# Head 1's last score product on the whole array, and every engine's order of instructions as a table

## The chip, the cores and the metric

The kernel runs on one core of one Trainium2 chip. The core's engines each work through their own queue of instructions in order: TensorE (PE) does matrix products into the accumulation memory PSUM, its weight loads are shown apart (PEld); VectorE (DVE), ScalarE (ACT) and GpSimd (POOL) do elementwise work and reductions; SyncE (SP) issues the DMA transfers. The metric is the device time of one execution in microseconds (us), the median of several runs; lower is better.

## The reference

Attention with queries pooled in twos, and then two projections multiplied with each other and projected back, on the attention's output as tokens:

```python
# batch, heads, sequence, head width = 4, 8, 1152, 64; tokens 2304 x 512; d_ff = 1536
q_pool = q.reshape(B, H, S // 2, 2, D).mean(axis=3)
scores = 1.0 / np.sqrt(D) * np.matmul(q_pool, k.transpose(0, 1, 3, 2))
scores = scores - np.max(scores, axis=-1, keepdims=True)
attn = np.exp(scores)
attn = attn / (np.sum(attn, axis=-1, keepdims=True) + 1e-09)
x = np.matmul(attn, v).transpose(0, 2, 1, 3).reshape(B * 576, 512)
out = ((x @ w_a) * (x @ w_b)) @ w_out
```

## The kernel before

**Tiling.** Heads are worked on in 16 pairs, four to a batch. Head 0 of a pair lies on partitions 0 to 63, head 1 on 64 to 127, so the scores of the two heads (64 deep) are products on the two row halves of PE's array. 128 queries of one head against 1152 keys are a *block*; there are 144. A *round* is the two blocks of a pair for the same 128 queries (the 64 queries that are left over in a pair make a round of their own, one block for both heads). Batch 0 goes through its pairs twice (first 256 queries of each pair, then the rest), batches 1 to 3 once: 20 passes with 80 rounds, 16 of which are such leftovers. In batches 0 and 1 scores are f32 products (line 563). In batches 2 and 3 (`ps_.split`) k and q are scaled and split into a high and a low f16 part (`k_hi`, `k_lo`, `q_hi`, `q_lo`), and each score is the sum of three f16 products (line 566).

**Scores in PSUM.** `sps` has five banks of 512 columns. Head 0's 1152 scores take the first two banks and 128 columns of the third; head 1's 1024 later keys take the last two banks and its first 128 keys another 128 columns of the third. The third bank is thus shared. `qk` does a round's five larger pieces in one task (512 and 512 for each head, 128 for head 0). Head 1's remaining 128 keys, piece (1, 3), are a task of their own, `qk_rest`, which waits (`after=(ps_.last_max,)`, line 635) until DVE has read head 0's scores (`sm_max`, line 593). A switch `whole` for doing it inside `qk` stands in `scores`, always False.

**A block after its scores.** `sm_max` (DVE, line 593, scaling and maximum), `sm_exp` (ACT, 600), `sm_sum` and `sm_rec` (DVE, 604 and 610), `sm_hi` (ACT, 613) and `sm_lo` (DVE, 617) make high and low f16 parts of the probabilities; a DMA transposes them (SP, 623); `pv` (PE, 652) multiplies them with v on column halves of the array. `x_copy`, `x_hi`, `x_lo` and `x_scale` (661, 682, 686, 692) bring the result into the form that the expert layers read.

**Expert layers.** Tokens are in nine groups t of 256: two for each batch, and group 8 from the leftovers of all batches. For each of 12 slices f of d_ff, `moe_mm` (730) makes two sums of 12 f16 products on the whole array, `moe_a` and `moe_g` (737, 742) scale and multiply them, `moe_gh` and `moe_gl` (747, 750) split the result into two f32r parts, and `moe_o` (756) does the output products on the whole array. Weights are loaded and split during the first four passes, staged in the tiles `z_t`, of which the third is `z2`.

**The order.** Nothing is issued where it stands. `add` records each piece as a task with its engine, a modelled duration, a key, what it reads and writes, and for PE a `mode` (0 whole array, 1 row halves, 2 column halves, 3 output products). `Plan.order` then runs a model of the five engines, picks the ready task with the lowest key, and repeats this after random shifts of the keys (`STEPS`, 63 settings); the tasks are emitted in the order of their modelled starts. On the chip every engine keeps that order, and semaphores do the waiting.

Of the kernel before, what the change touches and what calls it, by code (L numbers as in the profile page):

```python
# [56 lines left out]
STEPS = (  # L57
# [19 lines left out]
class Plan:  # L77
# [9 lines left out]
    def add(self, eng, dur, key, fn, args=(), r=(), w=(), gen=0.45, block=0.0, port=None, lag=0.0, after=(), mode=0):  # L87
# [14 lines left out]
        self.tasks.append((ENGINES.index(eng), dur, key, fn, args, sorted(deps), gen, block, eng == "POOL" if port is None else port, lag, mode))  # L102
        return n

    def run(self, key, back):

        eng, dur, lat, out, left, gen, block, port, lag, mode = self.back if back else self.forth
        n = len(eng)
        left = list(left)
        ready_at = [0.0] * n  # L110
        start = [0.0] * n
        free = [0.0] * len(ENGINES)
        dma_free = port_free = 0.0
        last = 0
        busy = {}
        waiting = [[] for _ in ENGINES]
        ready = [([], [], [], []) for _ in ENGINES]
        push, pop = heapq.heappush, heapq.heappop
        for i in range(n):
            if not left[i]:  # L120
                push(waiting[eng[i]], (0.0, i))
        for _ in range(n):
            best = None
            for e in range(len(ENGINES)):
                rd, q = ready[e], waiting[e]
                t = free[e]
                if q:
                    if not any(rd) and q[0][0] > t:
                        t = q[0][0]
                    while q and q[0][0] <= t:  # L130
                        i = pop(q)[1]
                        push(rd[port[i] if e != PE else mode[i]], (key[i], i))
                if e == PE:
                    from_ = min((x for x in rd if x), key=lambda x: x[0][0] - PE_STAY * (x is rd[last]), default=None)
                elif rd[1] and (not rd[0] or port_free <= t and rd[1][0] < rd[0][0]):
                    t, from_ = max(t, port_free), rd[1]
                else:
                    from_ = rd[0]
                if from_ and (best is None or t < best[0]):
                    best = (t, e, from_)  # L140
            t, e, from_ = best
            i = pop(from_)[1]
            t = max(t, ready_at[i])
            d = dur[i]
# [7 lines left out]
            else:  # L152
                end = t + d
                if e == PE:
                    if mode[i] != last:
                        d += PE_TURN
                        last = mode[i]
                    end = t + d
                    tick, at = int(t / PE_TICK), t
                    while True:  # L160
# [9 lines left out]
                        at = tick * PE_TICK  # L170
                free[e] = end
            start[i] = t
            le = lat[e]
            for j in out[i]:
                x = end + le[eng[j]]
                if x > ready_at[j]:
                    ready_at[j] = x
                left[j] -= 1
                if not left[j]:
                    push(waiting[eng[j]], (ready_at[j], j))  # L180
# [793 lines left out]
```

## Time and profile before

| | |
|---|---|
| median of 3 runs | 871.57 us (870.22 to 873.34) |
| profiled execution | 872.21 us, span from first to last instruction 870.4 us |
| mean granted PE clock | 0.947 of full speed |
| busy: PE, DVE, ACT, POOL | 782.0, 648.1, 577.3, 257.0 us |
| chain that ended last | PE 17% of the span, everything else 0% |

A profile is one execution. Busy time of an engine is the time in which one of its instructions ran; matrix products are pipelined, so those of PE overlap a little, and the time that a piece of work takes from PE is better read from its start to the start of what comes next. A timeline merges neighbouring instructions of one kind into one row with their count (x24). An f32 product shows as two instructions.

### The profile page before, as it was taken

How to read it: one execution, taken by the hardware profiler on the slowest of the kernel's cores; microseconds unless marked ns; L12 is line 12 of the kernel's file. 1: busy time of each engine (PE TensorE's matmuls, PEld its weight loads, DVE VectorE, ACT ScalarE, POOL GpSimd, SP SyncE). 2: the span in 40 equal slices, each digit the busy share in tenths (PEclk: the TensorE clock that was granted, in tenths of full speed). 3: DMA queues.
4: the chain of work that ended last, by engine and by line, in shares of the span. 5: the costliest groups of instructions: out<-in, count | busy, mean ns of one | idle time of the engine just before them, and what ended most of it. 6: DMA issues, size and time to landing. Idle time of an engine off the chain costs nothing. (4 is left out here: it accounts for less than half of the span.)

```text
span 870.4 us, 21299 instructions
## 1 busy us (share of the span) xinstructions
PE 782.0 (90%) x8832; PEld 588.2 (68%) x8832; DVE 648.1 (74%) x1240; ACT 577.3 (66%) x917; POOL 257.0 (30%) x228
## 2 busy tenths in 40 slices
PE   4665538999999999999999999999999999999997
PEld 2443315777667676678777777787778768888886
DVE  5999999989778889899888999898885763122010
ACT  5789787878767677777677787776774653233212
POOL 4459876520311102221031205210520221210303
PEclk9765757999999999999999999999999999999999
DMA  7999999899999999997989999988694564000100
GB/s 275 236 237 262 239 256 232 209 188 216 218 207 205 205 168 186 196 216 146 183 165 210 174 172 208 174 180 165 137 195 77 85 130 84 2 26 1 25 1 25
DMA packets 353665, 141.76 MB, mean 163 GB/s; under 512 B 338208, under 2 KB 340256, under 8 KB 353568
## 3 DMA queue, kind: packets, MB, share of 16 engines
q1 hardware_dynamic: 353568, 140.40, 80.2%
q8 instruction: 69, 1.13, 0.6%
q14 instruction: 28, 0.23, 0.1%
HBM read 50.72 MB, written 4.72 MB: 64 GB/s over the span
## 5 line engine op out<-in xcount | busy, mean ns | idle before, releaser
L730 PEld LDWEIGHTS <-wab 128*128 128x128 f16 x2592 | 249.2, 98 | 38.1 <-issue 1.8
L730 PE MATMUL ab<-xt,wab 128*128 128x256 f16 x2304 | 266.6, 274 | 1.7 <-DVE g L742 1.0
L617 DVE SCALAR_TENSOR_TENSOR p<-s,st,p 128x1152 f16<-128x1152 f32 x144 | 209.6, 1464 | 24.3 <-ACT p L613 23.9
L600 ACT ACTIVATE s<-s,st 128x1152 f32<-128x1152 f32 x144 | 180.0, 1250 | 66.9 <-DVE s L593 66.3
L613 ACT ACTIVATE p<-s,st 128x1152 f16<-128x1152 f32 x144 | 177.7, 1246 | 30.1 <-DMA pt<-p 17.4
L750 POOL TENSOR_TENSOR gl<-g,gh 128x256 fp32r<-128x256 f32 x108 | 90.2, 838 | 334.9 <-ACT gh L747 313.6
L563 PE MATMUL sps<-k,q 64*128 64x512 f32 (+3 forms) x480 | 124.6, 596 | 41.5 <-DVE s L593 31.6
L756 PE MATMUL ab<-wo,gh 128*128 128x512 f32 x432 | 141.6, 409 | 4.5 <-DVE g L742 2.4
L652 PE MATMUL xps<-pt,vs 128*64 128x128 f16 (+1 forms) x4320 | 126.4, 217 | 8.7 <-DMA pt<-p 5.6
L563 PEld LDWEIGHTS sps<-k,q 64*128 64x128 f32 (+1 forms) x480 | 58.7, 206 | 105.6 <-issue 57.9
L652 PEld LDWEIGHTS <-vs 128*64 128x64 f16 x4320 | 115.2, 112 | 21.9 <-issue 17.1
L737 ACT ACTIVATE g<-ab,cc 128x256 f32<-128x256 f32 (+1 forms) x144 | 55.6, 415 | 87.5 <-PE ab L730 87.2
L742 DVE SCALAR_TENSOR_TENSOR g<-ab,cc,g 128x256 f32<-128x256 f32 (+1 forms) x144 | 55.9, 411 | 77.5 <-ACT g L737 77.4
L593 DVE TENSOR_SCALAR_CACHE_REDUCE s<-sps,ksc 128x1152 f32<-128x1152 f32 x72 | 101.6, 1411 | 10.8 <-PE sps L566 10.7
L593 DVE TENSOR_SCALAR_CACHE_REDUCE s<-sps 128x1152 f32<-128x1152 f32 x72 | 97.0, 1348 | 13.3 <-PE sps L563 12.9
L756 PEld LDWEIGHTS ab<-wo,gh 128*128 128x128 f32 x432 | 77.5, 189 | 24.4 <-ACT gh L747 2.2
L756 PE MATMUL ab<-wo,gl 128*128 128x512 f32 x216 | 86.2, 399 | 0.1
L747 ACT ACTIVATE gh<-g 128x256 fp32r<-128x256 f32 x108 | 43.8, 411 | 53.1 <-PE ab L756 47.8
L566 PE MATMUL sps<-k,q 64*128 64x512 f16 (+3 forms) x720 | 76.4, 325 | 2.0 <-DVE s L593 1.9
L566 PEld LDWEIGHTS <-q 64*128 64x128 f16 (+1 forms) x720 | 36.5, 97 | 45.9 <-issue 16.4
L313 POOL TENSOR_TENSOR q<-qraw 128x576 f32<-128x576 f32 (+2 forms) x20 | 31.8, 1592 | 93.6 <-DVE q L350 30.3
L467 POOL TENSOR_SCALAR xt<-xt 128x512 f16<-128x512 f32 x22 | 53.1, 2413 | 20.4 <-ACT xt L463 19.2
(93 smaller groups left out, 613.7 us busy)
## 6 DMA issues: line engine op xcount, KB each, us to landing
vraw<-in_v_dram SPq DMA_DIRECT2D x19, 576.0 KB, 4.7
k<-in_k_dram SPq DMA_DIRECT2D x19, 576.0 KB, 4.8
xt<-in_w_ab_dram SPq DMA_DIRECT2D x15, 512.0 KB, 5.0
qraw<-in_q_dram SPq DMA_DIRECT2D x12, 576.0 KB, 4.9
out_dram<-o SPq DMA_DIRECT2D x16, 256.0 KB, 2.5
xt<-in_w_out_dram SPq DMA_DIRECT2D x7, 512.0 KB, 5.2
g<-in_w_ab_dram SPq DMA_DIRECT2D x5, 512.0 KB, 5.2
pt<-p SPq DMA_TRANSPOSE x144, 5.4
```

Of the source, the lines that this page charges most:

```text
L563: nc.tensor.matmul(out, qs[jq][rows, queries], kn[jk][rows, keys], start=True, stop=True)
L566: nc.tensor.matmul(out, qf[rows, hq - 1, queries], kf[rows, hk - 1, keys], start=(hq, hk) == (1, 1), stop=(hq, hk) == (2, 1),)
L593: nc.vector.tensor_scalar(out=s_t[sbuf(i)], in0=sps[:, at:at + S], scalar1=-1.0 / 16.0 if u is None else ksc[:, u, 4:5], scalar2=None, op0 ...
L600: nc.scalar.activation(out=s, in_=s, func=AF.Exp, scale=-1.0, bias=t[:, 0:1], accum_out=t[:, 1:2])
L613: nc.scalar.activation(out=p_t[pbuf(i)][:, 0], in_=s_t[sbuf(i)], func=AF.Copy, scale=st_t[i % NST][:, 3:4])
L617: nc.vector.scalar_tensor_tensor(out=p[:, 1], in0=s, scalar=st_t[i % NST][:, 3:4], in1=p[:, 0], op0=ALU.mult, op1=ALU.subtract)
L652: nc.tensor.matmul(xps[half(e), at:at + w], vs[:, c, e, hv], pt[:, hp, c, c0:c0 + w], start=(c == 0 and n == 0), stop=(c == NCH - 1 and n ...
L730: nc.tensor.matmul(dst if t < 8 else dst.rearrange("p (b n) -> p b n", b=B), wab[:, f, 1 - m, a, c], moe_x(t, b, c), start=(n == 0), stop= ...
L737: nc.scalar.activation(out=g_t[:, f, c], in_=ab[j][:, 1, c], func=AF.Copy, scale=cc[:, b, f, 0:1])
L742: nc.vector.scalar_tensor_tensor(out=g, in0=ab[j][:, 0, c], scalar=cc[:, b, f, 1:2], in1=g, op0=ALU.mult, op1=ALU.mult)
L750: nc.gpsimd.tensor_tensor(out=gl_t[j], in0=g_t[:, f], in1=gh_t[j].bitcast(F32), op=ALU.subtract)
L756: nc.tensor.matmul(acc[u], g[:, us], wo[:, f, a], start=(first and n == 0), stop=(last and n == 2))
```

## The change

Three things. First, in batches 1 to 3 `ps_.whole` is true, and for rounds of 128 queries head 1's first 128 keys are multiplied inside `qk`, as its last piece, on the whole array: the stationary operand is all 128 rows of q (both heads), the moving one a tile `kz` whose rows 0 to 63 are zero and whose rows 64 to 127 hold head 1's keys. The separate tasks for piece (1, 3) remain in batch 0 only. Second, what `kz` needs: two buffers within `z2`, cleared once on POOL after the weights (`kz_zero`), and one copy on ACT for each of 12 passes (`k_pad`). Third, `STEPS` and the search at build time are gone; `ORDERS` lists for each of PE, DVE, ACT, POOL and SP its tasks by number, in the order in which that engine is to do them; the numbers are those of the tasks in the order of the `add` calls. A task has a second mode, `leaves`, that is 0 for a round that ends on the whole array; the model with it now only merges the five lists.

```diff
-STEPS = (
-    (64937, 0.5, 225, 20, 2), (12302, 2.0, 678, 160, 1), (13399, 8.0, 513, 40, 2), (29057, 2.0, 604, 160, 2),
...
+ORDERS = (
+    (
+        13, 6, 21, 30, 38, 140, 148, 29, 157, 48, 165, 50, 67, 267, 94, 275, 121, 156, 284, 175, 292, 177, 394, 194,
...
+    def order(self):
+        n = len(self.tasks)
+        eng, dur, _, _, _, deps, gen, block, port, lag, mode, leaves = map(list, zip(*self.tasks))
...
+            for e, o in enumerate(ORDERS):
+                if pos[e] < len(o) and not left[o[pos[e]]]:
+                    i = o[pos[e]]
+                    t = max(free[e], ready_at[i], port_free if port[i] else 0.0)
+                    if best is None or t < best[0]:
+                        best = (t, e, i)
...
+    kz = [z_t[2][:, 128 * j:128 * j + 128] for j in range(2)]
+    kzf = [x.bitcast(F16).rearrange("p (a n) -> p a n", a=2) for x in kz]
...
+    def qk(ps_, rows, rest):
         pair = rows[0][2] == 128
...
+        whole = ps_.whole and pair
+        products = ((0, 0), (0, 1), (1, 0)) if ps_.split else (None,)
+        q, k, z = (qf, kf, kzf[ps_.z]) if ps_.split else (qs[ps_.jq], kn[ps_.jk], kz[ps_.z])
+        runs = [((0, 0), (1, 0)), ((0, 1), (1, 1)), ((0, 2),)] if pair else [[(0, m), (1, m)] for m in range(3)]
+        for run in [((1, 3),)] if rest else runs:
...
+        if whole:
+            c = rows[1][1]
+            for split in products:
+                product(sps[:, S_AT[1]:S_AT[1] + 128], split, q[:, ..., c:c + 128], z)
+
+    def kz_zero():
+        for x in kz:
+            nc.gpsimd.memset(x[half(0)], 0.0)
+
+    def k_pad(ps_):
+        if ps_.split:
+            nc.scalar.activation(out=kzf[ps_.z][half(1)], in_=kf[half(1), :, 0:128], func=AF.Copy)
+        else:
+            nc.scalar.activation(out=kz[ps_.z][half(1)], in_=kn[ps_.jk][half(1), 0:128], func=AF.Copy)
...
     def scores(ps_, i, rows, rest):
-        r, whole = kq_names(ps_), False
+        whole = ps_.whole and rows[0][2] == 128
+        r = kq_names(ps_) + [f"kz{ps_.z}"] * whole
         if not rest:
-            add("PE", (1.47 if ps_.split else 1.97) + whole * (0.16 if ps_.split else 0.3), i - 8, qk,
-                (ps_, rows, ps_.jk, ps_.jq, whole), r=r, w=["sps0", "sps1"], mode=1)
+            add("PE", (1.47, 1.73)[whole] if ps_.split else (1.97, 2.37)[whole], i - 8, qk, (ps_, rows, False), r=r,
+                w=["sps0", "sps1"], mode=1, leaves=0 if whole else 1)
         elif not whole:
-            add("PE", 0.16 if ps_.split else 0.3, i - 9, qk_rest, (ps_, rows, ps_.jk, ps_.jq), r=r, w=["sps1"],
+            add("PE", 0.16 if ps_.split else 0.3, i - 9, qk, (ps_, rows, True), r=r, w=["sps1"],
                 after=(ps_.last_max,), mode=1)
...
+            self.whole = b > 0
...
+        if ps_.whole and (ps_.split or not ps_.again):
+            add("ACT", 0.19, ps_.base - 8, k_pad, (ps_,), r=["kn1", "kn1l"] if ps_.split else [f"kn{ps_.jk}"], w=[f"kz{ps_.z}"])
...
+                if m == W_PASSES:
+                    add("POOL", 0.4, ps_.base, kz_zero, (), w=["z2", "kz0", "kz1"], port=False)
```

## Rows read from the trace of the kernel before

**Rows 1.** The page's first part: busy us (share of span) and instructions of PE.

```profile
PE 782.0 (90%) x8832; PEld 588.2 (68%) x8832; DVE 648.1 (74%) x1240; ACT 577.3 (66%) x917; POOL 257.0 (30%) x228
```

**Rows 2.** Windows: stretch; length, busy PE PEld DVE ACT POOL; PE clock, DMA, GB/s.

```profile
0.00:25.00 25.00, 9.44 (x26) 4.72 (x26) 14.33 (x28) 14.46 (x20) 12.85 (x11) 0.90 0.80 276
...
100.00:125.00 25.00, 9.46 (x92) 5.78 (x86) 24.86 (x55) 21.99 (x34) 19.65 (x10) 0.73 1.00 240
...
150.00:175.00 25.00, 23.79 (x307) 17.39 (x305) 23.51 (x53) 21.28 (x36) 12.93 (x9) 1.00 0.85 225
...
325.00:350.00 25.00, 23.39 (x298) 16.59 (x295) 23.05 (x40) 18.15 (x27) 5.69 (x6) 1.00 1.04 172
```

**Rows 3.** The chain that ended last, in order of time: start us, us, what.

```profile
816.91 31.60 PE ab L730 x288
...
849.58 17.08 PE ab L756 x72
```

**Rows 4.** Timeline of PE in batch 1: start, us, line, out<-in, shapes, count.

```profile
256.88 0.48 PE L563 MATMUL sps<-k,q 64*128 64x128 f32 x2
257.30 2.79 PE L730 MATMUL ab<-xt,wab 128*128 128x256 f16 x24
260.02 2.20 PE L563 MATMUL sps<-k,q 64*128 64x512 f32 x10
262.15 1.70 PE L652 MATMUL xps<-pt,vs 128*64 128x128 f16 x54
```

**Rows 5.** Timeline of PE in batch 2.

```profile
494.33 2.79 PE L730 MATMUL ab<-xt,wab 128*128 128x256 f16 x24
497.06 0.34 PE L566 MATMUL sps<-k,q 64*128 64x128 f16 x3
497.33 1.70 PE L652 MATMUL xps<-pt,vs 128*64 128x128 f16 x54
```

**Rows 6.** Groups by form, weight loads: shapes, count, busy us, mean ns, idle before.

```profile
L730 PEld LDWEIGHTS <-wab 128*128 128x128 f16 x2592 | 249.2, 98 | 38.1 <-issue 1.8 <-DVE g L742 1.0
...
L756 PEld LDWEIGHTS ab<-wo,gh 128*128 128x128 f32 x432 | 77.5, 189 | 24.4 <-ACT gh L747 2.2 <-issue 2.1 <-DVE g L742 1.4
...
L566 PEld LDWEIGHTS <-q 64*128 64x128 f16 x576 | 29.6, 94 | 39.3 <-issue 15.0 <-DVE st L604 0.4 <-ACT gh L747 0.2
```

**Rows 7.** Timeline of PE: separate products of head 1, with idle time and releaser.

```profile
289.26 0.49 PE L563 MATMUL sps<-k,q 64*128 64x128 f32 x2 [1.04 <-DVE s L593]
...
480.11 0.33 PE L566 MATMUL sps<-k,q 64*128 64x128 f16 x3 [0.52 <-DVE s L593]
```

**Rows 8.** Groups by form: copies of 64 columns, on ACT and on POOL.

```profile
L682 ACT ACTIVATE xr<-x 128x64 f16<-128x64 f32 x16 | 4.0, 249 | 0.2
...
L686 POOL TENSOR_TENSOR xr<-x,xr 128x64 f16<-128x64 f32 x16 | 7.1, 444 | 95.5 <-ACT xr L682 95.5
```

**Rows 9.** PE's waits from 200 us on: first, third, last of ten groups.

```profile
PE xps L323 <- ACT x L661: 3.2, 3, 1.4
...
PE ab L756 <- ACT gh L747: 2.0, 1, 2.0
...
PE ab L730 <- ACT o L764: 0.4, 1, 0.4
```

**Rows 10.** Timeline of PE and, last row, of DVE where the third group starts.

```profile
370.00 1.63 PE L566 MATMUL sps<-k,q 64*128 64x512 f16 x15
...
374.31 2.79 PE L730 MATMUL ab<-xt,wab 128*128 128x256 f16 x24
...
373.68 0.34 DVE L692 TENSOR_SCALAR xt<-xt,vsc 128x512 f16<-128x512 f16 x1
```

**Rows 11.** Timeline of PE: the first expert products and the fourteenth round.

```profile
142.55 2.72 PE L730 MATMUL ab<-xt,wab 128*128 128x256 f16 x12
...
150.21 2.20 PE L563 MATMUL sps<-k,q 64*128 64x512 f32 x10
```

**Rows 12.** The page's groups: DVE's subtraction in the softmax.

```profile
L617 DVE SCALAR_TENSOR_TENSOR p<-s,st,p 128x1152 f16<-128x1152 f32 x144 | 209.6, 1464 | 24.3 <-ACT p L613 23.9
```

More of the change, by code (lines that the diff above doesn't have):

```diff
@@ L101, in add @@
         deps.discard(n)
-        self.tasks.append((ENGINES.index(eng), dur, key, fn, args, sorted(deps), gen, block, eng == "POOL" if port is None else port, lag, mode))
+        self.tasks.append((ENGINES.index(eng), dur, key, fn, args, sorted(deps), gen, block, eng == "POOL" if port is None else port, lag, mode, mode if leaves is None else leaves))
         return n
[L105 to L112, printed above, removed]
-        dma_free = port_free = 0.0
[L114 to L122, printed above, removed]
-            best = None
[L124 to L144, printed above, removed]
@@ new lines, in order @@
+    def order(self):
+        n = len(self.tasks)
+        eng, dur, _, _, _, deps, gen, block, port, lag, mode, leaves = map(list, zip(*self.tasks))
+        assert all(eng[i] == e for e, o in enumerate(ORDERS) for i in o) and sorted(i for o in ORDERS for i in o) == list(range(n))
+        out = [[] for _ in range(n)]
+        for i in range(n):
+            for d in deps[i]:
+                out[d].append(i)
+        left = [len(x) for x in deps]
+        ready_at, start = [0.0] * n, [0.0] * n
+        free, pos = [0.0] * len(ENGINES), [0] * len(ENGINES)
+        dma_free = port_free = 0.0
+        last, busy, result = 0, {}, []
+        while len(result) < n:
+            best = None
+            for e, o in enumerate(ORDERS):
[4 more added lines that the diff above has]
+                        best = (t, e, i)
+            t, e, i = best
+            pos[e] += 1
+            result.append(i)
+            start[i], d = t, dur[i]
@@ L156, in run @@
                         d += PE_TURN
-                        last = mode[i]
+                    last = leaves[i]
                     end = t + d
@@ L558, in pbuf, with product @@
         return i % NPB
-    def product(out, split, jk, jq, rows, queries, keys):
+    def product(out, split, q, k):
         if not split:
-            nc.tensor.matmul(out, qs[jq][rows, queries], kn[jk][rows, keys], start=True, stop=True)
+            nc.tensor.matmul(out, q, k, start=True, stop=True)
         else:
             hq, hk = split
-            nc.tensor.matmul(
-                out, qf[rows, hq - 1, queries], kf[rows, hk - 1, keys],
-                start=(hq, hk) == (1, 1), stop=(hq, hk) == (2, 1),
-            )
@@ L571, in products @@
-    def products(ps_):
-        return ((1, 1), (1, 2), (2, 1)) if ps_.split else (None,)
-    def qk(ps_, rows, jk, jq, whole):
-        pair = rows[0][2] == 128
-        runs = [((0, 0), (1, 0)), ((0, 1), (1, 1)), ((0, 2),), ((1, 3),)] if pair else [[(0, m), (1, m)] for m in range(3)]
-        for run in runs if whole or not pair else runs[:3]:
-            qk_run(ps_, rows, jk, jq, pair, run)
-    def qk_rest(ps_, rows, jk, jq):
-        qk_run(ps_, rows, jk, jq, True, ((1, 3),))
-    def qk_run(ps_, rows, jk, jq, pair, run):
-        for split in products(ps_):
-            for j, m in run:
-                e, c, w = rows[j]
-                cuts, at, part = (S_CUT[e], S_AT[e], slice(0, 128)) if pair else (S_CUT[0], S_AT[0], half(e))
-                a, b = cuts[m:m + 2]
-                product(sps[part, at + a:at + b], split, jk, jq, half(e), slice(c, c + w), slice(a, b))
+            nc.tensor.matmul(out, q[:, hq], k[:, hk], start=(hq, hk) == (0, 0), stop=(hq, hk) == (1, 0))
@@ new lines, in qk @@
+    def qk(ps_, rows, rest):
+        pair = rows[0][2] == 128
+        whole = ps_.whole and pair
[4 more added lines that the diff above has]
+            for split in products:
+                for e, m in run:
+                    _, c, w = rows[e]
+                    cuts, at, part = (S_CUT[e], S_AT[e], slice(0, 128)) if pair else (S_CUT[0], S_AT[0], half(e))
+                    a, b = cuts[m:m + 2]
+                    product(sps[part, at + a:at + b], split, q[half(e), ..., c:c + w], k[half(e), ..., a:b])
+        if whole:
+            c = rows[1][1]
+            for split in products:
+                product(sps[:, S_AT[1]:S_AT[1] + 128], split, q[:, ..., c:c + 128], z)
@@ L857, in more @@
         ps_.end = len(blocks)
+        ps_.z = 0 if not passes else passes[-1].z if again and not ps_.split else 1 - passes[-1].z
         passes.append(ps_)
```

44 lines of the change are left out of this document (13 added, 31 removed), and 155 rows, old and new, of tables (ORDERS, STEPS).

## The prediction

> **What bounds the kernel now.** I read the page's header first, then busy time by stretch, then the chain of work that ended last, then TensorE's (PE's) order of work, and its waits. PE is busy for 782.0 of 870.4 us [rows 1]. The reader should see two regimes. In the first 150 us PE is half idle and VectorE (DVE) is not: from 100 to 125 us DVE is busy 24.86 of 25 us, PE 9.46 us at a mean granted clock of 0.73 [rows 2]. From 150 us on PE is nearly gapless at clock 1.00: 23.79 of the 25 us after 150, and 23.39 of those after 325, with DVE at 23.05 [rows 2]. The chain that ended last runs on PE through the last groups of the expert layers, 31.60 us of first products and then, a gap of about 1 us later, 17.08 us of output products [rows 3]. So after 150 us every microsecond of PE's own work that goes away is one of the end, as long as DVE, which has only 8% free in the middle, keeps up; before that, a shorter PE is worth nothing.
>
> **The change part by part.** Two edits go together: 48 small score products are done in another way, and every engine's order is new.
>
> *The turns of PE.* What stands in the rows is a cost of changing the form of the array. Products of the expert layers on the whole array run at 31.60 us for 288, that is 0.110 us each [rows 3]. Of these, 24 between an island of scores and a score round take from 257.30 to 260.02, 2.72 us, where 24 x 0.1097 = 2.63 were due: 0.09 us is the turn [rows 4]. In the f16 batches the same 24 take from 494.33 to 497.06, 2.73 us: 0.10 us [rows 5]. I take 0.092 for each turn. Following PE's instructions from the first product to the last and counting where the form changes (whole array; scores on row halves; values on column halves; output products, whose operands are f32r), I get 353 turns before; [rows 4, 5] show seven of them. After: the table's numbers are tasks in the order in which the add calls make them, so PE's row of the table can be read task by task. It has 220 turns between tasks and one inside each of the 48 score rounds that now end on the whole array, 268. That is 85 fewer, 85 x 0.092 = 7.8 us. The reason is plain in [rows 4, 5]: all 48 products of head 1's last 128 keys in batches 1 to 3 stand alone between work of another form (256.88, 497.06), paying a turn in and a turn out. Now they end their round: 32 of the 48 rounds are followed by whole-array work, which needs no turn out.
>
> *The products themselves.* Removed: 16 in f32, each from 256.88 to 257.30 = 0.42 less the turn out, 0.33 us [rows 4]; 32 in f16, three products each, 497.06 to 497.33 = 0.27 less the turn, 0.18 us [rows 5]. Together 16 x 0.33 + 32 x 0.18 = 11.0 us. Added are as many with 128 rows of weights instead of 64, same 128 columns. The trace has no such product, so it is bounded. Below: stream alone, half of the 0.110 us that 256 columns cost, three times, 0.16 us in f16; for f32 the round of 1152 columns takes 260.02 to 262.15 less a turn, 2.04 us, so 128 columns 0.23 us [rows 3, 4]: 8.8 us in all. Above: each weight load in series with its stream, 98 ns + 55 ns three times = 0.46 us, and two loads of 189 ns + 0.23 = 0.61 us in f32 [rows 6]: 24.5 us. The nearest row is the removed product itself: same moving columns and data types, and its loads are hidden, since three loads of 94 ns mean would alone take 0.28 us and the three products take 0.18 [rows 5, 6]. So I take 11.0 and the exchange is worth nothing by itself (-2.2 to +13.5 us).
>
> The Trainium skill, "TensorE: Matmul & The Clock Gate", Part 3 (The mechanism), speaks against the change: it has a weight load overlap products in flight only where the row groups differ, which a whole-array load never has. By that rule the sum takes the upper price, the second rival below; the trace does not bear it out where whole-array products of 256 columns follow one another, at 0.110 us with a load of 98 ns each [rows 3, 6].
>
> *Their waits.* Head 1's last product had to wait until DVE had read head 0's scores from the shared bank. After 200 us that shows twice on PE, 1.04 us at 289.26 and 0.52 us at 480.11 [rows 7]: 1.6 us that go. Nothing new is late in their place: the round already waits for both heads' reads, and the second read can follow the first at once.
>
> *Pads.* Twelve new copies on ScalarE (ACT) of 64 partitions by 128 (f32) or 256 (f16) elements; the nearest row is a copy of 64 columns, 249 ns [rows 8], so 12 x 0.25 = 3 us of an engine with 293 us free. Queued behind each are exponentials and copies of the softmax, and the first round of its pass waits for it; PE meanwhile has expert-layer products, which I let cover it. Without that cover, and with ACT waiting for DVE's split of k in eight passes, it is 3 to 5 us. GpSimd's two clears of 64 x 128 (nearest: 444 ns for 128 x 64 [rows 8]) wait for the last weight staged in z2. Behind them on POOL are a sum of q and the low halves of x for batch 0; POOL is the idlest engine. Nothing on either, 0.9 us (two clears) if the start of batch 1 waits for it. SyncE issues the same 256 transfers, and the DMA engines' work is unchanged.
>
> *The new order.* PE's row holds the same interleaving with small shifts: expert work ahead of each score round (12 first products at 0.110 us a task; 17.08 / 12 = 1.42 us an output task [rows 3]) differs by under 3 us for most of the 80 rounds, by 7 at the most. At the start it goes the other way: the table puts no expert product ahead of the fourteenth round, where the trace has them from 142.55 us and the round at 150.21 [rows 11], and two more DVE subtractions of the softmax (1.46 us each [rows 12]) and one more maximum of about that length, but one shorter weight subtraction less, ahead of the first multiplication of the expert layers (`moe_g`): some 4 us of DVE time; by the eighth of these the two orders stand within 1 us. So I count the first 150 us as even (-3 to +4). Later, PE's waits from 200 us on sum to 14.7 us in ten groups [rows 9]. Less the 1.6 counted, 13.1 are left; a new order can take all of them or add as many. I take 2.0, the longest single wait of the ten groups.
>
> *Sum.* The profiled execution took 872.2 us (span 870.4). 872.2 - 7.8 - 1.6 - 2.0 = 860.8. The median of the runs, 871.57, lies 0.6 below the profiled execution, so the forecast is 860.2 us.
>
> **The rivals.** (A) *PE waits for attention instead.* At 374.31 PE starts the third group of expert layers right after DVE's scaling of its input at 373.68 [rows 10]: the store of expert work from batch 0 has just run out, and every later batch has such a hand-over. If attention is set by DVE and its queue there, PE's saving only widens the gap, and what is left is the 1.6 us: 872.2 - 1.6 - 0.6 = 870.0. For: DVE at 92% [rows 2]. Against: it is PE that was busy up to the hand-over, and head 1's maximum no longer waits for PE.
>
> (B) *Slower: whole-array weight loads are not hidden.* Place: the end of each of the 48 rounds; price +13.5 us as above: 872.2 - 7.8 - 1.6 + 13.5 - 0.6 = 875.7. It decides from 0.20 us more per round on (9.4 / 48). Against it are the two rows named.
>
> (C) *The order itself is worth more.* If half of the other waits go (6.5 instead of 2.0) and the start gains 3 us, where in the first 25 us DVE is busy only 14.33 [rows 2], it is 860.2 - 7.5 = 852.7. Against: DVE is full by 100 us, and an order written from modelled times leaves waits where the chip differs.
>
> **How the numbers follow.** Forecast 0.68, A 0.14, B 0.08, C 0.10. The forecast's own spread is 854.5 to 866 (order -4 to +6 about it). 80% needs some of A and C: 853 to 869. Faster by over 0.3% (under 869, about what a measurement can tell): forecast, C and the part of A that loses only some of the saving, 0.81; within 0.3%: 0.11; slower: B, 0.08.
>
> **What would show it.** Right: no score product of 128 columns stands alone after batch 0; expert products before a round's end keep 0.110 us; the rounds of batches 2 and 3 grow from 1.6 [rows 10] to about 1.9 us with the inner turn and whole product, and those of batch 1 from 2.1 to about 2.5 [rows 4]; PE's busy time falls by some 8 us; the clock is 1.00 from 150 us on. Wrong: rounds over 2.0 us in f16 (B); PE gaps of several us before the third, fifth and seventh group with DVE as releaser (A); the first expert product later than 146 us (the start); waits after 200 us that sum to over 15 us (the order).

## The result and the profile after

The changed kernel takes 851.38 us, median of 4 runs (850.55 to 853.44), against 871.52 before: a ratio of 0.9771, 95% interval 0.9745 to 0.9797. That is 20.1 us less, where the prediction had 11.4 less and a range from 853 to 869; the time lies just below the range, nearest to rival C (852.7). The profiled execution took 852.03 us, its span is 849.8.

Header and windows of the changed kernel, columns as in [rows 1, 2]; the last window is longer:

```profile
PE 771.8 (91%) x8832; PEld 591.2 (70%) x8832; DVE 644.9 (76%) x1240; ACT 580.9 (68%) x929; POOL 255.1 (30%) x230
...
100.00:125.00 25.00, 10.21 (x32) 4.72 (x30) 24.30 (x56) 22.24 (x34) 19.43 (x10) 0.68 0.92 217
150.00:175.00 25.00, 23.09 (x310) 17.90 (x308) 22.03 (x45) 18.57 (x33) 17.28 (x10) 1.00 0.99 245
325.00:350.00 25.00, 25.00 (x306) 17.83 (x303) 22.42 (x44) 18.59 (x30) 8.02 (x11) 1.00 1.06 194
250.00:720.00 470.00, 468.13 (x6002) 364.38 (x6002) 400.85 (x735) 349.04 (x534) 93.85 (x107) 1.00 0.92 171
```

PE's busy time is 10.2 us lower than in [rows 1]. The first 175 us look as they did. What is new comes later: from 325 to 350 us PE has no gap at all (23.39 before), and from 250 to 720 us 1.9 us of gaps in 470. The same window of the kernel before, for comparison, left 10.5:

```profile
250.00:720.00 470.00, 459.49 (x5867) 346.30 (x5866) 401.87 (x733) 340.76 (x511) 94.10 (x104) 1.00 0.93 171
```

Note the counts: in the same 470 us PE does 135 more products (6002 against 5867).

PE's waits after the change, from 200 us to the end: engine, line, what it waited for; us in total, times, longest:

```profile
PE ab L830 <- DVE g L842: 2.1, 1, 2.1
PE ab L856 <- DVE g L842: 1.7, 2, 1.3
PE sps L657 <- issue: 1.0, 1, 1.0
PE xps L752 <- DMA pt<-p: 0.7, 1, 0.7
```

Four groups and 5.5 us stand where [rows 9] had ten groups and 14.7 us. Between 250 and 720 us only the last two are left.

The new rounds on PE, one of batch 1 (f32) and one of batch 2 (f16): start, us, line, out<-in, shapes, count:

```profile
288.05 2.17 PE L657 MATMUL sps<-k,q 64*128 64x512 f32 x10 [0.97 <-issue]
290.16 0.49 PE L657 MATMUL sps<-z,q 128*128 128x128 f32 x2
290.48 4.09 PE L830 MATMUL ab<-xt,wab 128*128 128x256 f16 x36
...
558.11 1.63 PE L660 MATMUL sps<-k,q 64*128 64x512 f16 x15
559.67 0.34 PE L660 MATMUL sps<-z,q 128*128 128x128 f16 x3
559.85 4.09 PE L830 MATMUL ab<-xt,wab 128*128 128x256 f16 x36
```

The products on the whole array (128*128) end their round, and expert products follow at once. From start to start the two f32 pieces take 0.32 us (290.16 to 290.48) and the three f16 pieces 0.18 us (559.67 to 559.85): what the separate products of [rows 4, 5] took without their turns, 0.33 and 0.18. The 36 expert products behind them start 0.112 us apart (559.85 to the next round at 563.88), turn included.

The chain that ended last, share of the span by engine, first after and then, in a fence of its own, before:

```profile
PE 53%; DVE 2%; DMA 1%; issue 1%; ACT 0%
```

```profile
PE 17%; ACT 0%; DVE 0%; issue 0%; DVEq 0%
```

Before, the chain can be followed back only to 712.63 us, the last 18% of the span. After, it goes back through more than half of it, nearly all on PE. The second line was on the page when the prediction was made.

**Where the 20 us went.** To see this I priced PE's tasks: each kind by the time from its start to the next task's start where PE is gapless, and 0.093 us for each change of array form. The rest of the span is idle time (in the first 150 us it includes the lower clock). The transfer records give the moment at which the last of the 144 transposes of probabilities has landed, which is when attention has nothing more to fetch.

| | span | PE's work | last transpose landed | PE's work left then | idle ahead of it | idle behind it |
|---|---|---|---|---|---|---|
| before | 870.4 | 739.1 | 730.4 | 133.0 | 124.3 | 7.0 |
| after | 849.8 | 731.2 | 731.9 | 111.8 | 112.5 | 6.1 |

Attention ends at nearly the same time in both. What differs is how much expert work is still to be done then: 21.2 us less, and 21.2 - 1.5 + 0.9 = 20.6, the difference of the spans. By these prices the 21.2 us come from ahead of the landing: 7.9 us were turns and are now work, 11.8 us were idle and are now work, 1.5 us are the later landing.

The table is an account, not a cause. The same sum comes out at any moment behind which PE has hardly a gap, and PE does not wait for the last landing in either kernel: it takes up the last two products with v at 746.41 and 751.03 us before, behind 288 first products without a gap, and at 726.57 and 736.79 us after. Nor does PE's row move 21 us of expert work. When the last score round starts, at 711.29 us before and 695.91 after, about 147 and 143 us of expert products are left (counted in the traces, 0.109 us for a first and 0.237 for an output product). Some 4 us are thus the row's, and 15.4 us are PE getting there sooner. What tells the kernels apart is how long attention can hold PE up. PE's last listed wait for it, before (a timeline row, then the chain):

```profile
711.29 1.62 PE L566 MATMUL sps<-k,q 64*128 64x512 f16 x15 [1.39 <-DVE s L593]
...
714.88 31.60 PE ab L730 x288
746.48 1.63 PE xps L652 x54
```

And after (the chain; the wait is the 0.7 us for a transpose in the list above):

```profile
371.85 6.33 DMA pt<-p
378.18 0.04 issue
378.22 1.67 PE xps L752 x53
```

Before, PE waits for attention here and there up to 711 us. After, it does so up to 378 us; the three waits listed from there on lie within the expert layers.

### The profile page after: what moved, and what is told of

Its sections match the earlier page's. It is cut to its first block, busy times and chain, and to the rows that moved or that the text cites. A ratio compares the mean times of both kernels' runs of the same rounds, so it can differ in the third digit from the quotient of the medians.

```text
span 849.8 us, 21268 instructions
## 1 busy us (share of the span) xinstructions
PE 771.8 (91%) x8832; PEld 591.2 (70%) x8832; DVE 644.9 (76%) x1240; ACT 580.9 (68%) x929; POOL 255.1 (30%) x230
## 4 chain that ended last, share of the span: by engine, by line
PE 53%; DVE 2%; DMA 1%; issue 1%; ACT 0%
PE ab L830 24%; PE ab L856 14%; PE sps L660 8%; PE xps L752 7%; DMA pt<-p 1%; DVE p L716 1%; DVE s L692 1%; DVE g L842 0%; ACT g L837 0%; PE xps L485 0%; DVE vs L518 0%; DVE vmx L481 0%; DVE o L862 0%; PE xps L418 0%; DVE st L709 0%
## 5 line engine op out<-in xcount | busy, mean ns | idle before, releaser
L830 PEld LDWEIGHTS <-wab 128*128 128x128 f16 x2592 | 252.4, 98 | 35.2 <-issue 2.3
L830 PE MATMUL ab<-xt,wab 128*128 128x256 f16 x2304 | 262.3, 274 | 3.2 <-DVE g L842 3.2
L716 DVE SCALAR_TENSOR_TENSOR p<-s,st,p 128x1152 f16<-128x1152 f32 x144 | 206.7, 1439 | 20.1 <-ACT p L712 19.4
L850 POOL TENSOR_TENSOR gl<-g,gh 128x256 fp32r<-128x256 f32 x108 | 94.0, 877 | 328.9 <-ACT gh L847 295.0
L657 PE MATMUL sps<-k,q 64*128 64x512 f32 (+3 forms) x448 | 117.5, 620 | 56.5 <-DVE s L692 36.6
L657 PEld LDWEIGHTS sps<-k,q 64*128 64x128 f32 (+1 forms) x448 | 54.0, 210 | 118.8 <-issue 62.9
L752 PEld LDWEIGHTS <-vs 128*64 128x64 f16 x4320 | 117.8, 113 | 19.3 <-issue 16.0
L856 PEld LDWEIGHTS ab<-wo,gh 128*128 128x128 f32 x432 | 77.8, 188 | 20.1 <-ACT g L837 1.5
L660 PE MATMUL sps<-k,q 64*128 64x512 f16 (+3 forms) x624 | 65.4, 341 | 0.0
L856 PEld LDWEIGHTS ab<-wo,gl 128*128 128x128 f32 x216 | 40.6, 188 | 10.1 <-POOL gl L850 0.4
```

The costliest lines, as they stand in the source:

```text
L657: nc.tensor.matmul(out, q, k, start=True, stop=True)
L660: nc.tensor.matmul(out, q[:, hq], k[:, hk], start=(hq, hk) == (0, 0), stop=(hq, hk) == (1, 0))
L716: nc.vector.scalar_tensor_tensor(out=p[:, 1], in0=s, scalar=st_t[i % NST][:, 3:4], in1=p[:, 0], op0=ALU.mult, op1=ALU.subtract)
L752: nc.tensor.matmul(xps[half(e), at:at + w], vs[:, c, e, hv], pt[:, hp, c, c0:c0 + w], start=(c == 0 and n == 0), stop=(c == NCH - 1 and n ...
L830: nc.tensor.matmul(dst if t < 8 else dst.rearrange("p (b n) -> p b n", b=B), wab[:, f, 1 - m, a, c], moe_x(t, b, c), start=(n == 0), stop= ...
L850: nc.gpsimd.tensor_tensor(out=gl_t[j], in0=g_t[:, f], in1=gh_t[j].bitcast(F32), op=ALU.subtract)
```

## The experiments

Ratios are against the kernel before, on the same chip and with 95% intervals; "against the change" is the difference to 0.9771, taken of 871.5 us. "Old order" is the order of the kernel before, engine by engine, written down as a table. The kernels that keep the old tasks are made from the source of the change with `whole` false and a table for these tasks. Landing, work left and span are from each kernel's own profiled execution, which can lie up to 5 us off its median.

### Each part alone

*The products alone*: the change's `qk`, pads and clears, with the old order of every engine (the 48 separate products dropped from PE's row). PE's row of the table:

```diff
-        402, 411, 419, 221, 248, 283, 619, 302, 305,
+        402, 411, 221, 419, 248, 619, 283, 302, 628,
...
```

> The old order of every engine, unchanged, with the 48 separate products of batches 1 to 3 taken out and head 1's last piece done on the whole array at the end of its round; the 12 pads stand ahead of their pass's first round. Theory 1 (the table removed PE's waits; the whole-array product only saved turns): PE's work falls by 7.9 us and the two waits of the separate products go, but the other waits after 250 us stay, so about 862 us. Theory 2 (the whole-array product removed the waits, because head 1's maximum no longer waits for PE and attention gets ahead of PE): nearly all of the change's gain, 852 to 855 us, with the table adding little. Theory 3 (the old order does not fit the new tasks): waits on the pads, no gain or a loss, 868 us or more.

Measured: 872.76 us, 1.0024 (1.0001 to 1.0048). No gain. Its waits on PE from 250 to 720 us, the four largest groups of thirteen:

```profile
PE xps L726 <- DMA pt<-p: 5.1, 5, 1.8
PE xps L392 <- ACT x L735: 2.4, 2, 1.7
PE sps L634 <- DVE s L666: 2.1, 2, 1.7
PE sps L631 <- DVE s L666: 2.0, 4, 0.6
```

PE's work did fall by 4.4 us at the prices above (739.1 to 734.7; 304 turns, since the old neighbours of a round are mostly of another form), and its idle time rose by 6.8. PE arrives earlier at the products with v and waits there for the transposes: 5.1 us, where the same wait before the change was 0.9 us. This is rival A's mechanism, and in the old order it takes everything.

*The order alone*: the table of the change with the old 48 separate products, each put into PE's row where the changed kernel's trace shows head 0's maximum to be done. Where the table takes head 1 ahead of head 0, the two products keep their old sequence.

```diff
-            self.whole = b > 0
+            self.whole = False
```

> The table's order with the old score method: the 48 products separate again, each placed in PE's row where the trace of the changed kernel shows head 0's maximum to be done; no pads; where the table reads head 1 first, head 0 first. Theory 1 (the table removed the waits): the changed kernel's time plus the 7.9 us of turns plus a few us of waits of the separate products, 859 to 864 us. Theory 2 (the whole-array product removed them): 867 us or more, with the waits after 250 us back at the old 14 us or so.

Measured: 901.01 us, 1.0331 (1.0292 to 1.037). PE's waits from 200 us on, the three largest groups:

```profile
PE sps L635 <- DVE s L667: 11.2, 12, 1.8
PE ab L805 <- DVE g L817: 8.2, 6, 2.6
PE sps L632 <- DVE s L667: 7.8, 5, 3.6
```

The order doesn't fit the old tasks. PE hardly waits at the separate products (64x128); it waits at the next rounds (64x512) until DVE has read the scores. The f16 groups by form, 200 to 900 us (busy us, mean ns; idle before):

```profile
L635 PE MATMUL sps<-k,q 64*128 64x512 f16 x384 | 47.7, 380 | 8.0 <-DVE s L667 7.9
L635 PE MATMUL sps<-k,q 64*128 64x128 f16 x192 | 21.5, 219 | 0.7 <-DVE s L667 0.7
```

That the late second product delays head 1's maximum, and this the next round, is argued from it. The places of the 48 products were chosen for this run, and others were not tried. So it doesn't price the order by itself; together with the run before it shows that in these forms neither part gains anything without the other.

### What a microsecond of PE's work is worth in either order

*The whole-array pieces done twice and left out* (in the second one head 1's first 128 keys of batches 1 to 3 get no scores), both in the change:

```diff
-        if whole:
+        for _ in range(2 * whole):
```

```diff
-        if whole:
+        for _ in range(0 * whole):
```

> The changed kernel with each of the 48 whole-array pieces done twice, the second over the first; nothing else differs. Added on PE are 32 x 0.18 + 16 x 0.32 = 10.9 us. Theory 1 (PE alone sets the time after 150 us and the order has no slack): all of it shows, about 862 us. Theory 2 (attention's chain through DVE and ACT sets parts of it): well under half shows, 851 to 856 us.

> The changed kernel without the 48 whole-array pieces: the scores of head 1's first 128 keys in batches 1 to 3 are not computed, everything else stays, in the changed order. PE loses 32 x 0.18 + 16 x 0.32 = 10.9 us. Theory 1 (in the changed order PE alone sets the time, in both directions): 11 us less, a ratio of 0.965 to the kernel before. Theory 2 (the fixed order has attention close behind PE, so that work taken away from PE turns into waits, as with the old order and whole-array products): 5 us less or under, 0.971 or more.

Measured: 861.8 us, 0.9888 (0.9856 to 0.992), and 843.33 us, 0.9696 (0.967 to 0.9721). The pieces are 10.9 us of PE's work. A second set adds less than was reckoned, since it follows the first without a start of its own: in its trace the f16 pieces take 0.34 us instead of 0.18 (564.76 to 565.10) and the f32 pieces 0.55 instead of 0.32 (289.33 to 289.88), 9.0 us in all. It costs 10.2 us against the change, one for one; taking the set away gives 6.5. Each of these two differences is uncertain by some 3 to 4 us.

*The separate products done twice*, in the kernel before, for batches 1 to 3:

```diff
-        for run in [((1, 3),)] if rest else runs:
+        for run in [((1, 3),)] * (2 if ps_.p // NP > 0 else 1) if rest else runs:
```

> The old kernel in its order with each of the 48 separate products done twice, the second over the first. Added on PE are 16 x 0.33 + 32 x 0.18 = 11.0 us, and head 1's maximum waits that much longer each time. Theory 1 (the old order, too, shows PE's work one for one when work is added): a ratio of 1.012. Theory 2 (the old order's waits take it up): under 1.006.

Measured: 872.16 us, 1.0017 (0.9996 to 1.0039). Here, too, the second product adds less than was reckoned: 0.42 us became 0.64 in f32 (255.12 to 255.76) and 0.27 became 0.44 in f16 (494.21 to 494.65). PE was given 9.0 us more to do and the kernel took 1.5 us more. The window of this kernel, columns as in [rows 2]:

```profile
250.00:720.00 470.00, 463.52 (x5974) 351.94 (x5975) 400.38 (x728) 339.31 (x508) 95.05 (x103) 1.00 0.92 170
```

PE is busier by 4.0 us and, over the whole span, idle for some 8 us less; DVE's and ACT's work in the window is what it was. PE is the busiest engine here and yet had some 8 us to give away.

*Waits alone*: old order, but the sums of k for passes 12, 14 and 15 (`xps`, line 323) go one PE task later, past what they waited behind; these are the 3.2 us at the head of [rows 9].

```diff
-1257, 1205, 901,
+1257, 901, 1205,
...
-1461, 1418, 1771, 1774,
+1461, 1771, 1418, 1774,
...
-1814, 1518, 1571,
+1814, 1571, 1518,
```

> The old kernel and its order, with three instructions of PE moved: the sums of the maxima of k for passes 12, 14 and 15, which had PE wait 1.37, 1.20 and 0.65 us for ACT's copy of x, stand one PE task later. Theory 1 (a wait of PE after 150 us is worth its length at the end, and an order alone removes it): 3 us less, about 868.5 us. Theory 2 (a wait removed comes back as another one later, because attention is as critical as PE): no change, 871.5 us.

Measured: 871.09 us, 1.0013 (0.9991 to 1.0035). Nothing: the three waits are gone from its trace, that for transposes has grown from 0.9 to 2.3 us, and the largest group of PE's waits was worth none of its microseconds.

### What paces attention

Three cuts, each made in the kernel before and in the change. (1) DVE: the low part of the probabilities isn't made for the last 128 keys in 108 of the 144 blocks, 17 us of DVE. (2) ACT: the same for the high part, 12 us of ACT. (3) Transfers: 24 loads of k and v bring 512 of 1152 keys, 7.9 MB less (132.5 instead of 140.4). (4) All three, in the kernel before. The edits of DVE and of the loads of k are shown; those of ACT and of v are alike.

```diff
+        n = S if i < 36 else S - 128
-            out=p[:, 1], in0=s, scalar=st_t[i % NST][:, 3:4], in1=p[:, 0], op0=ALU.mult, op1=ALU.subtract
+            out=p[:, 1, 0:n], in0=s[:, 0:n], scalar=st_t[i % NST][:, 3:4], in1=p[:, 0, 0:n], op0=ALU.mult, op1=ALU.subtract
```

```diff
-        nc.sync.dma_start(out=kn[j], in_=k[p])
+        n = S if p < NP else 512
+        nc.sync.dma_start(out=kn[j][:, 0:n], in_=k[p][:, 0:n])
```

> The old kernel in its order; in the 108 blocks of batches 1 to 3 DVE's subtraction in the softmax leaves out the last 128 of 1152 keys (their low parts keep older values). DVE loses 108 x 0.16 = 17 us of work, PE nothing. Theory 1 (in the old order attention's chain through DVE paces PE's fixed order, which is why PE's own work counts little there): 8 us less or more, a ratio of 0.990 or under. Theory 2 (PE's queue and its waits on something else set the time): under 3 us, 0.997 or more.

> The same cut in the changed kernel. Theory 1 (in the changed order PE sets the time, and DVE's chain runs ahead of it): 4 us less at the most against the changed kernel, a ratio of 0.973 or more to the kernel before; a larger loss would say that DVE paces the changed kernel as well.

> The old kernel in its order; in the same 108 blocks ACT's copy of the probabilities leaves out the last 128 keys (older values stay). ACT loses 108 x 0.11 = 12 us, DVE and PE nothing. If the pace is that of the whole round trip scores, maximum, exponential, copy, subtraction, transpose: 5 us less or more, 0.994 or under. If it is DVE's queue alone: under 3 us, 0.997 or more.

> The same cut in the changed kernel. If PE sets the time there: within 2 us of the changed kernel, a ratio of 0.975 to 0.979.

> The old kernel in its order; in batches 1 to 3 the 24 loads of k and v bring only 512 of 1152 keys (the others keep older values): 7.7 of 141 MB less, in loads that lie between the transposes. In every run of the old order so far the last transpose landed at 726 to 733 us and 133 us of PE's work plus 7 us were left behind it. If the transfers pace attention there: the last transpose 8 us earlier or more, a ratio of 0.991 or under. If not: 0.996 or more, as with the cuts on DVE and ACT.

> The same cut in the changed kernel, where 112 us of PE's work are left behind the last transpose. If PE paces attention there: within 3 us of the changed kernel, 0.973 to 0.979. If the transfers do: 0.970 or under.

> The old kernel in its order with the three cuts together: 17 us less on DVE, 12 us on ACT, 7.7 MB less of transfers, PE unchanged. If attention's pace is one engine's: about the largest of the single gains. If it is the fixed order itself, each engine waiting in turn for the others: about their sum or more. If PE's own queue limits it, together no more than the 27 us that PE idles after 250 us, and PE's idle time there is what shrinks.

| cut | in the kernel before | in the change |
|---|---|---|
| DVE | 868.49, 0.9968 (0.994 to 0.9995) | 849.44, 0.9751 (0.9703 to 0.98) |
| ACT | 870.13, 0.998 (0.9956 to 1.0005) | 849.87, 0.975 (0.9706 to 0.9793) |
| transfers | 862.75, 0.9916 (0.9898 to 0.9935) | 849.41, 0.976 (0.974 to 0.978) |
| all three | 862.25, 0.991 (0.9889 to 0.993) | not run |

In the old order it is the transfers that pay: 7.3 us, with DVE's cut 2.8, ACT's 1.7 (not told from nothing), and all three no more than the transfers alone. In the new order no cut gives 2 us, the transfers about 1. The kernel before with fewer transfers, columns as in [rows 2]:

```profile
250.00:720.00 470.00, 463.79 (x5940) 352.40 (x5938) 401.75 (x731) 341.29 (x514) 95.83 (x105) 1.00 0.87 159
```

The DMA share falls from 0.93 to 0.87, and PE, which was given nothing and lost nothing, is busier by 4.3 us of the window. Its last transpose lands at 720.5 us, 9.9 earlier, and the work left then is the same 133.0 us. From 225 to 730 us the median time from issue to landing falls from 5.2 to 4.9 us for a transpose, and for the loads themselves from 4.6 (k) and 4.7 (v) to 3.0 and 3.5. Both got faster, and this run doesn't tell which of them pays.

### What the order is worth, and how exactly

In these runs the orders were searched again or shaken, by small moves of tasks in the engines' rows, judged by the kernel's own model of its engines. A line of PE's row stands for each.

*Searched anew from the old order*, first with the old tasks, then, with the same effort, with those of the change; and the change's table searched on from where it stands.

```diff
-67, 267, 94, 275, 284, 121, 156,
+67, 94, 267, 121, 275, 284, 156,
...
```

> The old score method, the 48 products of batches 1 to 3 separate as before and no pads; only the order of every engine is new, found by ten minutes of small random shifts in the five lists from the old order, judged by the kernel's own model of the engines. PE's row has 310 turns instead of 353, so its work is about 735 us against 739 before and 731 in the changed kernel. Theory 1 (the order carries the gain, the whole-array products only some turns): PE's idle time falls as in the changed kernel, by 10 us or more, and the time is 853 to 858 us. Theory 2 (the whole-array products are what lets an order close the waits): idle stays within 5 us of before, 864 us or more.

> The changed kernel's score method with an order found in the same way, from the old order with the separate products taken out (which ran in 872.8 us). 248 turns, PE's work about 729.5 us. Theory 1 (a fixed order must be fitted anew to each set of tasks, and then the saved turns show too): 4 to 8 us under rest_searched, at or under the changed kernel, 846 to 853 us. Theory 2 (the old order's waits come from its start, which small shifts don't leave): 860 us or more.

> The changed kernel with its table shifted on in the same way for ten minutes; 254 turns. PE's work about 730 us. Theory 1 (the model of the engines still points the right way where the table ends): 845 to 850 us. Theory 2 (what is left is where the model and the chip differ): 851 us, no change, or slower.

Measured: 862.1 us, 0.9916 (0.9882 to 0.995); 858.25 us, 0.9871 (0.9839 to 0.9904); 858.49 us, 0.987 (0.9831 to 0.9909). With an order searched for them, the old tasks gain some 7 us, and the new ones some 4 more, though these two intervals overlap. The third one is the warning: the model gave it 834.1 us where it gives the change's table 840.6, and it is slower by 9 us. The same model gives the two orders searched from the old one 837.2 and 829.8 us, better than the change, and the chip puts them 13 and 9 us behind it.

*Shaken at the same modelled time*: 4000 moves from the change's table, none of which raised the modelled time by more than 0.26 us; first on all engines, then on all but PE.

```diff
-29, 157, 48, 165, 50, 67, 94,
+29, 48, 157, 165, 50, 67, 94,
...
```

> The changed kernel's table after 4000 small random shifts in the five lists, none of which may raise the modelled time by over 0.26 us: tasks stand 0.3 (PE) to 2.2 (DVE) places from where they stood, PE's row has 270 turns instead of 268. Theory 1 (what closed the waits is the order as the model sees it): the changed kernel's time within 3 us, a ratio of 0.977 to 0.981. Theory 2 (much of the gain lies in details of this one table that the model cannot tell apart): 5 us or more is lost, 0.983 or more.

> The same with PE's row kept as it is; only the rows of DVE, ACT, POOL and SP are shifted. Theory 1: as the changed kernel, 0.977 to 0.981. Theory 2: if walk_all loses and this one loses as much, the details that count are in the order of DVE, ACT and the transfers; if this one keeps the time, they are in PE's row.

Measured: 862.59 us, 0.9911 (0.9883 to 0.9938), and 857.97 us, 0.9855 (0.9827 to 0.9882). In the first one PE's tasks stand 0.3 places from where they were on average, DVE's 2.2; that costs 12 us. With PE's row untouched it costs 7. Neither beats the change, nor did any other kernel that does all of the work.

### All of them in one view

| kernel | last transpose landed | PE's work left then | span |
|---|---|---|---|
| before | 730.4 | 133.0 | 870.4 |
| products alone, old order | 732.6 | 133.2 | 872.8 |
| separate products twice | 731.3 | 133.1 | 871.4 |
| sums of k later | 727.7 | 133.1 | 867.8 |
| before, less DVE | 726.1 | 133.4 | 866.6 |
| before, less ACT | 725.7 | 133.0 | 865.7 |
| before, less transfers | 720.5 | 133.0 | 860.5 |
| before, less of all three | 719.4 | 133.5 | 859.9 |
| after | 731.9 | 111.8 | 849.8 |
| whole pieces twice | 739.0 | 111.8 | 857.0 |
| whole pieces left out | 723.7 | 111.7 | 841.6 |
| after, less DVE | 728.8 | 111.9 | 846.8 |
| after, less ACT | 729.4 | 111.9 | 847.4 |
| after, less transfers | 730.7 | 111.7 | 848.6 |
| order alone | 782.2 | 111.7 | 900.0 |
| old tasks, searched | 739.4 | 115.3 | 862.4 |
| new tasks, searched | 726.3 | 120.1 | 854.2 |
| table searched on | 749.6 | 104.9 | 861.8 |
| shaken, all | 741.6 | 109.8 | 858.3 |
| shaken, not PE | 734.6 | 115.0 | 855.9 |

In each row the span is the landing, plus the work left, plus 6 to 8 us of idle time; this holds by construction, since PE has hardly a gap behind the landing. The work left is read at the place that PE has reached in its row when the last transpose lands. The landing is what the chip makes of all five rows of the table together. An order with less work left is not better by itself (104.9, but 749.6): PE does the work earlier, and attention may pay for it. As long as the order stays, the work left does too (133 in the old one, 112 in the change), and what a cut or an addition does shows in the landing alone.

## Why the prediction was right or wrong

**Right: the turns.** 85 fewer were counted from the table, 7.8 us. The trace after has 267 against 353, 86 fewer. That PE's work is 7.9 us smaller checks the count and not the price, which went into it. Turns out of output products are dearer than the price: 12 of these take 2.99 us (748.11 to 751.10 before) where 60 without a turn inside take 14.20, so 0.15 us. And [rows 4, 5] show five turns, not seven.

**Right: the exchange of the products**, 11.0 for 11.0. Measured are 0.32 us for the f32 pair and 0.18 us for the f16 three, so 16 x 0.32 + 32 x 0.18 = 10.9. (The f16 round with its piece grew to 1.74 us, 558.11 to 559.85, not to about 1.9: the 1.6 from which that was reckoned already held a turn.) Rival B, with 0.20 us more per round as its turning point, is out. The Trainium skill, "TensorE: Matmul & The Clock Gate", Part 3 (The mechanism), lists among its rules that weight loads overlap products in flight only where the row groups differ; a few lines earlier it also allows it for a load into the background weight buffer. Here whole-array pieces follow one another within 0.06 us although each f16 piece has a load of 98 ns, so the measurement decides against the rule as the prediction took it.

**Right: the pads and the start.** The twelve copies take 0.31 us in f32 and 0.41 in f16, 4.5 us in all where 3 were reckoned (ACT's busy time rose by 3.6 us), and no PE wait names them. At the start, the sign that the prediction had named did show up: the first expert product comes at 147.1 us, later than 146 and than 142.55 in [rows 11]:

```profile
143.33 3.86 PE L657 MATMUL sps<-k,q 64*128 64x512 f32 x10 [3.69 <-DVE s L692]
147.12 1.48 PE L830 MATMUL ab<-xt,wab 128*128 128x256 f16 x12
```

It cost little: PE's idle time up to 250 us is 106.8 us against 104.4, inside the -3 to +4 that was given. The clock was not 1.00 all the way from 150 us on: 0.93 from 200 to 225 us, as it had been 0.98 and 0.95 from 225 to 275 us before.

**Wrong: the order's term.** The prediction took 1.6 us of waits for the separate products and 2.0 us for the order, 3.6 in all. PE's listed waits after 200 us fell from 14.7 to 5.5 us, that is 9.2, and its idle time after 250 us in the account above from 26.9 to 11.8, that is 15.1 us. The sum with the terms of the account is -7.9 + 2.4 - 15.1 = -20.6, the difference of the spans. The term was bounded on its good side by the 13.1 us of listed waits, but its value was taken from one single wait, with nothing that favoured 2 over 10, and rival C's half of the waits with 3 us at the start was given a chance of 0.10 only. The idle time of the account is larger than what the trace shows: PE's gaps after 250 us, short ones included, fell from 13.0 to 3.5 us, and some 3.8 us at the end are in both. The rest is in the prices, as for the turns out of output products. If every product is priced by its mean time to the next start between the same neighbours in the 20 traces, the three terms come out as some -9.3, +1.1 and -12.4. Either way the order's term was several times too small.

**Wrong, and more important: the premise behind the sum.** "After 150 us every microsecond of PE's own work that goes away is one of the end" is not true of the old order. There 9.0 us more work cost 1.5, the products alone gave nothing, and 3.2 us of listed waits gave nothing. In the new order it is nearly true: +10.2 for +9.0, -6.5 for -10.9. So the terms don't add, and the saved turns are worth nothing unless the order puts other work where they were. What the turns are worth in the new order can be estimated from the two runs on it: 7.9 us at 6.5 per 10.9, or one for one, 4.7 to 7.9 us. The remaining 12 to 15 us of the 20.1 are the order's, for these tasks.

**Rival A was right about the old order, with the wrong place and engine.** It looked for PE's wait at the start of the third, fifth and seventh group, with DVE as the releaser, and took DVE's 92% for its sign [rows 2]. In the run with the products alone the wait appeared at the products with v, and its releaser was the transposes; cutting transfers paid 7.3 us and cutting DVE 2.8. A hint stood in the same rows, a DMA share of 1.04 from 325 to 350 us, which the prediction did not read; but it is no sign by itself, as the change has 1.06 there and gains only about 1 us from fewer transfers. The better sign was in [rows 3], by what the chain lacks: it ends in the last expert groups, which the prediction took for proof that PE paces everything from 150 us on, but the chain of that page covers 17% of the span on PE and says nothing about what came before 712 us.

The Trainium skill, "Perfetto Trace Analysis", section "Identifying the Most-Contended Engine", picks the engine to work on by its occupancy; for TensorE it holds the busy share of matmuls a poor measure of the distance to the peak and offers, besides the rate of arithmetic, the busy share of weight loads. That share, 68% before and 70% after, doesn't tell the two kernels apart, and neither does PE's busy share, 90% and 91%. Adding work did: 1.5 us against 10.2.

**What stays open.** Cutting DVE, ACT and transfers together brings the kernel before to 862.25 us, no further; what holds its attention then was not found. Nor was it settled what makes this table better than its neighbours: the kernel's model rates them equal or better, and the chip puts them 7 to 12 us behind. That shaking the other engines alone costs 7 us says that much of it lies in the order of DVE, ACT, POOL and SP, not in PE's. The model ranks these three rightly (893 us for the order alone, 860.2 for the products alone, 840.6 for the change), but not the orders that were searched by it. Whether a table fitted to the old tasks with the same effort would come nearer than 862.1 was not tried; how much effort stands behind the change's table is not known.

## What to carry to other kernels

A busy engine is not the one that paces the kernel: before its work is priced one for one, follow the chain of waits back and see how much of the span it covers, or give the engine some extra work and look whether the time moves. Where several engines work through fixed orders, find the last moment at which the busy engine waits for another stream: work saved ahead of it can turn into longer waits, work saved behind it counts. Beware of accounts that add up at any moment, such as landing plus work left: they locate a gain and don't explain it. A part that gives nothing in the old order may still be worth its price in an order made for it, so try it with the order searched anew, and measure: a model that agrees on large differences can mislead a search.

## What was unexpected of the hardware

Whole-array products directly behind products on row halves showed no cost beyond the turn, which the round ahead of them holds (1.56 us, 558.11 to 559.67): three f16 pieces of 128 columns in 0.18 us. The page's groups show them with no idle time ahead (busy us and mean ns of one; idle before):

```profile
L660 PE MATMUL sps<-z,q 128*128 128x128 f16 x96 | 10.9, 223 | 0.0
L657 PE MATMUL sps<-z,q 128*128 128x128 f32 x32 | 7.8, 326 | 0.0
```

Their means of 223 and 326 ns overlap one another: 96 products at 0.06 us are 5.8 us of PE's time, not 10.9. And transfers can hold back a kernel whose PE is 90% busy: with 7.9 MB taken out of 24 of its loads, of 140.4 MB of traffic, the transposes landed earlier and 7.3 us came back. That the loads delay the transposes on the DMA engines that they share is argued from this and from the medians above, not shown; the loads' own earlier landing may pay as well.
